# Decode attention with a gated FFN: the last 128 KB of the output weights loaded in rows of 124 and 4

## Chip, cores, metric

One core of a Trainium2 chip. The metric is the device time of one execution in microseconds. Times inside an execution are microseconds from the start of the profile's span.

## The reference, cut

```python
q = (x @ wq)                                   # x: 4 x 512, one decode step, 32 heads of 128
k, v = k_cache[:, :, -4096:, :], v_cache[:, :, -4096:, :]     # 8 KV heads
o = softmax(q k^T / sqrt(128)) v               # cut
a = o.reshape(4, 1, 4096) @ wo                 # wo: 4096 x 512, bf16, 4 MB
b = (relu(x W_gate) * (x W_up)) @ W_down
out = g * a + (1 - g) * b                      # g = sigmoid(x . gate_w)
```

81 MB are read from HBM for four rows of output.

## The kernel before

All loads are issued by SyncE, in one order: `wq`, small inputs, the K and V windows in pieces of 4 MB, the FFN's weights, and at the end `wo` in six pieces, each with a semaphore of its own. A row of `Wo` on a partition is 32 blocks (`i`) of 512 elements (1 KB); a piece `(lo, hi)` is that range of blocks on all 128 partitions.

```python
WO_PIECES = ((0, 8), (8, 16), (16, 24), (24, 28), (28, 30), (30, 32))
# ... in the sync program
elif k == "wo":
    lo, hi = WO_PIECES[it[1]]
    load(("WO", it[1]), f"d_wo{it[1]}", Wo[:, lo:hi, :], A_wo.rearrange("(p i) c -> p i c", i=32)[:, lo:hi, :], waits=w)
# ... in the tensor program: two matmuls per block, accumulated in one bank
def WO(p):
    lo, hi = WO_PIECES[p]
    w = [("WO", p)] + [("E", "OQ", g) for g in range(2)]
    for i in range(lo, hi):
        for j in range(OUTT):
            mm(...)            # cut: oq[:, i, :] against Wo[:, i, 256 j : 256 j + 256]
# ... after the last of them VectorE evicts the bank and SyncE and ScalarE store it
```

## Time and profile before

| | before |
|---|---|
| time, median of 3 runs | 197.48 us |
| span of the profiled run | 195.6 us |
| PE, DVE busy | 62%, 63% |
| DMA | 415 GB/s on average |

Two lines of the page, the span in 40 equal slices of 4.9 us: the busy share of the 16 DMA engines in tenths, and what they moved.

```profile
DMA  6999999999999999999999999999999999999991
GB/s 221 442 423 436 429 442 436 419 436 429 436 456 429 437 426 436 429 429 429 436 429 436 426 429 429 429 429 429 429 426 429 429 405 434 448 429 403 417 402 53
```

From the second slice to the last but one the engines are 90% or more busy. No compute engine comes near that over the span.

The end of the chain of waits (start, length, what):

```profile
173.35 19.49 DMA slots<-in_A_wo_dram
192.84 0.04 issue
192.89 0.40 PE bank L320 x4
193.29 0.02 issue
193.31 0.42 DVE osum L576
```

The last load was issued at 173.35 us and landed at 192.84; everything after it is four short matmuls (0.40 us), one eviction and the store. So what this tail costs is decided by when the **last engine** has delivered.

The DMA view, queues (packets, MB, share of the 16 engines' time) and the loads of `wo` (KB each, us to landing):

```profile
q1 hardware_dynamic: 3904, 81.01, 97.1%
q8 instruction: 6, 0.10, 0.2%
q14 instruction: 1, 0.01, 0.0%
...
slots<-in_A_wo_dram SPq DMA_DIRECT2D x3, 1024.0 KB, 16.4
...
slots<-in_A_wo_dram SPq DMA_DIRECT2D x1, 512.0 KB, 19.2
slots<-in_A_wo_dram SPq DMA_DIRECT2D x2, 256.0 KB, 19.4
```

Besides the loads (q1) there are seven packets that fetch instructions. They look negligible, 0.2%. They are not, for a reason that no average shows.

**From packets to engines.** The packet records have start, duration and size, but no engine. A packet nearly always starts 3 or 4 ns before its predecessor on the same engine ends, so packets can be chained into 16 engines, by a search for the cheapest consistent assignment. Chains are not equally certain: where two run within a few ns of each other they can be swapped. What follows uses only what all best assignments share. Of the kernel before, the start of each engine's last semaphore write (us), with the instruction fetches that its chain holds:

```
ten engines without a fetch         190.46 to 191.11
fetch of  8 KB (q14) at  63.7       191.96
fetches of 16 KB (q8) at 39.1, 72.0, 110.9, 146.0, 182.6     192.11 192.36 192.29 192.24 192.28
```

A chain that took a fetch falls 1.0 to 1.6 us further back, against the middle one, and stays there to the end, within 0.3 us: no engine idles, so none catches up. Only part of that is the fetch's own packet (0.31 us for 8 KB, 0.92 to 1.06 for 16 KB). The 32 KB packet behind it took 1.71 to 1.87 us, where 1.21 is usual (behind the fetch at 182.6 an 8 KB packet, 0.81 instead of 0.31). The landing of 192.84 us belongs to one of those six. (A seventh fetch, at 191.5 us, left no delay in any chain: its engine was through or nearly so.)

### The profile page before, as it was taken

What the parts mean: (1) busy time and instruction counts of PE and PEld (TensorE: products, weight loads), DVE (VectorE), ACT (ScalarE), POOL (GpSimd) and SP (SyncE); (2) the same over time, 40 slices, a digit from 0 to 9 for tenths busy, and PEclk for the clock granted to TensorE, in tenths of its full rate; (3) what the DMA queues carried; (4) which work ended last, traced back from release to release, by engine and by line L of the source; (5) the groups of instructions that cost most, each with busy time, mean ns of one, the idle gap of its engine ahead of it and who ended that gap; (6) DMA issues with size and microseconds to landing.
All of it is one profiled execution on the core that took longest, in us unless ns stands there. A gap on an engine that the chain in (4) does not pass through costs nothing.

```text
span 195.6 us, 1780 instructions
## 1 busy us (share of the span) xinstructions
PE 121.2 (62%) x741; PEld 50.9 (26%) x741; DVE 124.0 (63%) x153; ACT 27.3 (14%) x33; POOL 9.5 (5%) x25
## 2 busy tenths in 40 slices
PE   0418279465933894595468953893395557734954
PEld 0213123122411331142113521241141112412631
DVE  6104769999299819971998199819972997460000
ACT  2213000040130013001300131014001400420100
POOL 7830000000000000000000000000000000000000
PEclk9999957999999697999886999699999789997999
DMA  6999999999999999999999999999999999999991
GB/s 221 442 423 436 429 442 436 419 436 429 436 456 429 437 426 436 429 429 429 436 429 436 426 429 429 429 429 429 429 426 429 429 405 434 448 429 403 417 402 53
DMA packets 3919, 81.12 MB, mean 415 GB/s; under 512 B 572, under 2 KB 584, under 8 KB 968
## 3 DMA queue, kind: packets, MB, share of 16 engines
q1 hardware_dynamic: 3904, 81.01, 97.1%
q8 instruction: 6, 0.10, 0.2%
q14 instruction: 1, 0.01, 0.0%
q10 hardware_dynamic: 8, 0.00, 0.0%
HBM read 81.01 MB, written 0.00 MB: 414 GB/s over the span
## 4 chain that ended last, share of the span: by engine, by line
DMA 54%; DVE 30%; PE 9%; issue 5%; SPq 1%; ACT 0%
DMA slots<-in_A_k_cache_dram 38%; DVE kt L492 21%; DMA slots<-in_A_wo_dram 10%; PE bank L320 7%; DMA gwT<-in_gate_w_dram 6%; DVE sc L528 5%; DVE qblk L518 1%; SPq L256 1%; DVE pT L543 1%; PE bank L324 1%; DVE rd L532 1%; ACT gwB L598 0%; DVE negmax L538 0%; DVE oq L555 0%; DVE osum L576 0%
## 5 line engine op out<-in xcount | busy, mean ns | idle before, releaser
L492 DVE STREAM_TRANSPOSE kt<-slots 128x2048 f32<-128x2048 f32 x32 | 73.7, 2304 | 27.5 <-DMA slots<-in_A_k_cache_dram 27.5
L320 PE MATMUL bank<-kt,qblk 128*128 128x512 bf16 x256 | 71.4, 430 | 29.2 <-DVE kt L492 29.1
L320 PEld LDWEIGHTS bank<-kt,qblk 128*128 128x128 bf16 x256 | 24.9, 106 | 70.7 <-DVE kt L492 37.6
L320 PE MATMUL bank<-slots,pT 128*64 128x512 bf16 x256 | 32.0, 407 | 5.7 <-DMA slots<-in_A_v_cache_dram 5.7
L617 ACT ACTIVATE pe<-sc,negmax 128x2048 bf16<-128x2048 bf16 x8 | 16.0, 2002 | 60.3 <-DVE negmax L538 60.3
L528 DVE CUSTOM_DVE_ANT_0 sc<-bank,maskf 128x512 bf16<-128x512 f32 x32 | 21.1, 658 | 4.1 <-PE bank L320 4.1
L320 PEld LDWEIGHTS bank<-slots,pT 128*64 128x64 bf16 x256 | 15.0, 117 | 23.1 <-issue 13.1
L543 DVE STREAM_TRANSPOSE pT<-pe 128x2048 bf16<-128x2048 bf16 x8 | 18.5, 2312 | 2.2 <-ACT pe L617 2.2
L602 ACT ACTIVATE osb<-bank 128x512 bf16<-128x512 f32 x8 | 4.8, 597 | 81.5 <-PE bank L320 81.5
L320 PE MATMUL bank<-rd,grpb 128*128 128x32 bf16 x8 | 1.5, 192 | 21.0 <-DVE rd L532 19.3
L555 DVE TENSOR_TENSOR oq<-bank,recip 64x128 bf16<-64x128 f32 x2 | 0.9, 442 | 11.5 <-PE bank L320 11.4
L320 PEld LDWEIGHTS bank<-rd,grpb 128*128 128x128 bf16 x8 | 0.8, 97 | 24.7 <-DVE rd L532 22.7
L320 PE MATMUL bank<-slots,oq 128*4 128x256 bf16 x64 | 4.3, 272 | 2.6 <-DMA slots<-in_A_wo_dram 1.9
L496 DVE COPY xT<-bank 128x16 bf16<-128x16 bf16 x1 | 0.2, 167 | 8.2 <-PE bank L324 8.2
L320 PE MATMUL bank<-slots,xT 128*4 128x512 bf16 (+1 forms) x64 | 5.2, 483 | 0.0
L576 DVE CAST osum<-bank 128x256 bf16<-128x256 f32 x1 | 0.4, 425 | 6.5 <-PE bank L320 6.5
L518 DVE TENSOR_SCALAR qblk<-bank 32x64 uint32<-32x64 uint32 x16 | 2.9, 215 | 2.3 <-PE bank L324 2.2
L320 PE MATMUL bank<-maskr,maskl 128*128 128x512 bf16 x1 | 0.6, 609 | 5.9 <-POOL maskr L296 5.9
L324 PE MATMUL bank<-identb,xsb 4*128 4x4 bf16 x4 | 0.3, 166 | 5.4 <-DMA xsb<-in_A_x_dram 5.4
L320 PEld LDWEIGHTS bank<-slots,oq 128*4 128x4 bf16 x64 | 2.3, 83 | 4.4 <-DMA slots<-in_A_wo_dram 3.1
L296 POOL TENSOR_SCALAR_AFFINE_SELECT fold<-fold 128x256 bf16<-128x256 bf16 x8 | 3.3, 417 | 1.1
L487 DVE MEMSET qblk<- 128x2304 uint32 x1 | 2.0, 1978 | 1.4 <-PEq L640 1.4
(58 smaller groups left out, 42.2 us busy)
## 6 DMA issues: line engine op xcount, KB each, us to landing
slots<-in_A_k_cache_dram SPq DMA_DIRECT2D x8, 4096.0 KB, 25.2
slots<-in_A_v_cache_dram SPq DMA_DIRECT2D x8, 4096.0 KB, 30.6
slots<-in_A_wq_dram SPq DMA_DIRECT2D x1, 4096.0 KB, 12.4
slots<-in_A_wo_dram SPq DMA_DIRECT2D x3, 1024.0 KB, 16.4
slots<-in_B_W_gate_dram SPq DMA_DIRECT2D x1, 1792.0 KB, 19.7
slots<-in_B_W_up_dram SPq DMA_DIRECT2D x1, 1792.0 KB, 23.6
slots<-in_B_W_down_dram SPq DMA_DIRECT2D x1, 1792.0 KB, 18.6
slots<-in_A_wo_dram SPq DMA_DIRECT2D x1, 512.0 KB, 19.2
```

The costliest lines, as they stand in the source:

```text
L256: E.op(lambda: e.dma_start(dst, src), ev=ev, waits=waits, ctr=ctr)
L296: op(lambda: e.affine_select(dst, src, pattern, cmp, fill, base=base, channel_multiplier=mult), ev)
L320: E.op(lambda: t.matmul(out_, lhsT, rhs, start=start, stop=stop, tile_position=pos, skip_group_check=True), ev=ev, waits=waits)
L324: E.op(lambda: t.transpose(out_, in_, idn), ev=ev, waits=waits)
L487: E.op(lambda: v.memset(qblk[:, :, :, :, :].rearrange("p s h c e -> p (s h c e)"), 0.0), ev=("QZ",))
L492: E.op(lambda: v.transpose(kt[:, f, :].bitcast(FP32), slot("k", s)[:, 4096 * f:4096 * f + 4096].bitcast(FP32)), ev=("E", "KT", s, f), waits=w)
L518: E.op(lambda dst=dst, r=r, g=g: v.tensor_scalar(dst, src[r, g, 0:B, :, :], 0, None, op0=ALU.bitwise_or), ev=("E",) + keys[1] if (q, g) == ...
L528: E.op(lambda: v.tensor_tensor_reduce(sc[:, 512 * f:512 * f + 512], banks[scb(key)], R["maskf"][:, :], 1.0, -3.0e38, ALU.add, ALU.max, mx4 ...
L532: E.op(lambda: v.tensor_tensor(rd32[:, :, :], bc(R["own8"][:, :].unsqueeze(2), 2, 4), bc(mx4[:, :].unsqueeze(1), 1, 8), ALU.mult), ev=("MA ...
L543: E.op(lambda: v.transpose(pT[:, s % 2, :], pe[:, :]), ev=("E", "PT", s), waits=[("EXP", s)] + ([("PV", s - 2)] if s >= 2 else []))
L602: E.op(lambda: a.activation(osb[:, s % 4, :], ob(s), ACTF.Copy), ev=("NORM", s), waits=[("PV", s)] + ([("OQ", 0)] if s >= 4 else []))
L617: E.op(lambda: a.activation(pe[:, :], sc[:, :], ACTF.Exp, bias=negmax[:, s % 2:s % 2 + 1], scale=SCALE, accum_out=rowsum[:, s:s + 1]), ev= ...
```

## The change

Its intent, as far as the diff tells it: let the last 128 KB be carried by four engines, so that the other twelve, the late ones among them, finish earlier.

```diff
-WO_PIECES = ((0, 8), (8, 16), (16, 24), (24, 28), (28, 30), (30, 32))
+WO_PIECES = ((0, 8), (8, 16), (16, 24), (24, 28), (28, 30), (30, 31), (31, 32))
+LOW4 = (0, 124, 128)
...
+    def wo_rows(p):
+        return [slice(a, b) for a, b in zip(LOW4, LOW4[1:])] if p == len(WO_PIECES) - 1 else [slice(0, 128)]
...
-                load(("WO", it[1]), f"d_wo{it[1]}", Wo[:, lo:hi, :], A_wo.rearrange("(p i) c -> p i c", i=32)[:, lo:hi, :],
-                     waits=w)
+                wo = A_wo.rearrange("(p i) c -> p i c", i=32)
+                for n, r in enumerate(wo_rows(it[1])):
+                    load(("WO", it[1], n), f"d_wo{it[1]}_{n}", Wo[r, lo:hi, :], wo[r, lo:hi, :], waits=w)
...
-            w = [("WO", p)] + [("E", "OQ", g) for g in range(2)]
+            w = [("WO", p, n) for n in range(len(wo_rows(p)))] + [("E", "OQ", g) for g in range(2)]
```

## The prediction

> **What bounds it now.** The page's slices show the DMA engines 90% or more busy from slice 2 to 39 at about 429 GB/s, and the chain of waits ends in the loads of the output weights: 19.5 us from the issue at 173.35 us, then the last four matmuls (0.40 us), the eviction (0.42 us) and the store. So only the moment when the last output weights land counts. DVE and PE (63%, 62% busy) are not the limit there.
>
> **The tail, engine by engine.** The trace records each DMA packet with start, duration and size. A packet starts 3 to 4 ns before its predecessor on the same engine ends, so I chained them into 16 engines. Just before the last 256 KB piece (8 rows of 2 KB each per engine) ten engines are early and six late by about 1 to 1.3 us; they write their last semaphore from 190.46 to 191.11 us (ten) and from 191.96 to 192.36 us (six). The six are those that each served one instruction fetch (16 KB packets near 39, 72, 111, 146 and 183 us, one of 8 KB near 64 us); one fetch puts an engine back by 1.0 to 1.45 us for good. The landing that PE waits for, 192.84 us, is a late engine's.
>
> **What the change does.** The last piece becomes two: 128 KB as before on 16 engines, 128 KB in rows of 124 and 4. The Trainium skill ("DMA: Bandwidth & Descriptors", on why a DMA increments its semaphore by 16) says that a DMA uses the largest number of engines up to 16 that divides its rows, the lowest-numbered ones: 4 for both. The trace agrees for a 4-row load: x has one semaphore update at issue and four at landing.
>
> Costs, from packets: a 2 KB row occupies an engine for 80 ns, a 1 KB row 42 ns (46 less the overlap).
> - Twelve engines: 8 x 80 becomes 8 x 42 ns: 0.30 us earlier.
> - Four lowest: 8 + 31 + 1 rows of 42 ns instead of 8 of 80: 1.68 against 0.64 us, 1.05 us later.
> - Two further issues of 0.43 us end near 174.3 us, 16 us before their data: free. One more wait on PE: free. Last matmuls: two instead of four, some 0.07 us less.
>
> **Critical path.** If all four lowest engines were early ones they would end near 191.8 us, still before the other late ones (192.07), and the kernel would gain 0.3 us. But the chains in which the four 1 KB packets of x lie (the four lowest) include, in every reconstruction that fits, the one of the 8 KB fetch at 64 us, which is late: its second last piece ends at 191.32 us. From there 40 rows take 1.70 us: 193.02 us instead of 192.37 us. So +0.65 us, less 0.07: about +0.6 us on 197.48, **198.1 us**. Range 197.3 to 198.9: lower if no late engine is among the four, higher if a 16 KB fetch has hit one of them too (two of the four are ambiguous), or the fetch at 191.5 us does.
> Chances: faster by over 2% 0.005, within 2% 0.98, slower by over 2% 0.015.
>
> **What will show it.** Landings of the 124-row and the 4-row load: one update group at issue, four at landing, the last near 193.4 to 193.5 us; packets of 1 KB on only four chains after about 192.1 us; all before 189 us unchanged; the last matmul group starts near 193.5 us and has two matmuls.
>
> **What would make it wrong.** Fetches that fall on other engines from run to run; four engines that slow each other (packets well over 46 ns), which would cost up to another microsecond; or 1 KB rows that cost more than x's did.

## The result

| | before | changed |
|---|---|---|
| median (6 runs each) | 197.36 us | 197.89 us |
| lowest to highest | 197.31 to 197.48 | 197.81 to 198.23 |
| span of the profiled run | 195.6 us | 196.2 us |

The ratio is 1.0028, 95% interval 1.0016 to 1.0041. (A ratio is the mean time of one kernel's fast runs over that of the other's fast runs of the same rounds, so not quite the ratio of the medians.) The changed kernel is slower by 0.5 us, and the interval leaves out 1.

The same views of the changed kernel. The slices:

```profile
DMA  6999999999999999999999999999999999999990
GB/s 220 434 429 434 441 434 454 441 431 428 434 428 434 429 428 424 428 428 428 428 428 428 424 434 428 441 428 428 428 444 428 441 400 456 434 404 413 423 370 28
```

Only the end differs, and little can be read from it: a slice is a fortieth of the span, so the last ones begin some 0.6 us later in the changed kernel. Over equal stretches the two move nearly the same: 392 and 387 GB/s from 188 to 190 us, 247 and 243 from 190 to 192, 14 and 11 from 192 to 194. The engines have to be looked at one by one.

The end of the chain of waits:

```profile
174.07 19.42 DMA slots<-in_A_wo_dram
193.49 0.14 issue
193.62 0.29 PE bank L326 x2
193.91 0.02 issue
193.94 0.42 DVE osum L582
```

The last landing is 0.65 us later (193.49 against 192.84), the matmuls behind it are 0.11 us shorter because two are left instead of four, and PE idles 0.14 us after the landing before it starts them, instead of 0.04. The eviction is as long as before.

The DMA view:

```profile
q1 hardware_dynamic: 4040, 81.01, 96.8%
q8 instruction: 6, 0.10, 0.2%
q14 instruction: 1, 0.01, 0.0%
...
slots<-in_A_wo_dram SPq DMA_DIRECT2D x1, 128.0 KB, 19.4
slots<-in_A_wo_dram SPq DMA_DIRECT2D x1, 124.0 KB
...
slots<-in_A_wo_dram SPq DMA_DIRECT2D x1, 4.0 KB
```

The two new loads have no time to landing: the view gives one only for a load with 16 semaphore updates from the engines. These two have one update at issue and four at landing. The landings of the last loads (us), and the last semaphore write of the chains:

```
16-engine load, 128 KB   190.65 ... 192.64   (16 updates)
124 rows                 174.19, then 192.11 192.51 192.59 193.30
4 rows                   183.88, then 192.29 192.68 192.78 193.49

chains with 40 rows of 1 KB at the end, fetch of 8 KB at 64.6   192.87
chains with 40 rows of 1 KB at the end, no fetch                191.57 192.04 192.08
chains with a fetch of 16 KB                                    191.79 to 192.04
other chains                                                    190.09 to 190.83
```

Here the four are certain, since only they carry 1 KB rows to the end. One of them is the late one, and it lands 0.7 us after the other three.

### The profile page after: what moved, and what is told of

Same layout as the page of the kernel before. It is cut to its first block, busy times and chain, and to the rows that moved or that the text cites. A ratio compares the mean times of both kernels' runs of the same rounds, so it can differ in the third digit from the quotient of the medians.

```text
span 196.2 us, 1783 instructions
## 1 busy us (share of the span) xinstructions
PE 124.0 (63%) x741; PEld 52.5 (27%) x741; DVE 124.3 (63%) x153; ACT 27.3 (14%) x33; POOL 9.6 (5%) x25
## 4 chain that ended last, share of the span: by engine, by line
DMA 41%; DVE 31%; PE 19%; issue 6%; SPq 2%; ACT 0%
DMA slots<-in_A_k_cache_dram 25%; DVE kt L498 21%; PE bank L326 17%; DMA slots<-in_A_wo_dram 10%; DMA gwT<-in_gate_w_dram 6%; DVE sc L534 5%; SPq L261 2%; PE bank L330 2%; DVE qblk L524 1%; DVE pT L549 1%; DVE rd L538 1%; DVE negmax L544 0%; ACT gwB L604 0%; DVE oq L561 0%; DVE osum L582 0%
## 5 line engine op out<-in xcount | busy, mean ns | idle before, releaser
L326 PE MATMUL bank<-slots,pT 128*64 128x512 bf16 x256 | 33.4, 420 | 5.7 <-DMA slots<-in_A_v_cache_dram 5.7
L326 PEld LDWEIGHTS bank<-slots,pT 128*64 128x64 bf16 x256 | 15.5, 121 | 23.9 <-issue 14.5
```

Source lines behind the costliest of these rows:

```text
L326: E.op(lambda: t.matmul(out_, lhsT, rhs, start=start, stop=stop, tile_position=pos, skip_group_check=True), ev=ev, waits=waits)
```

## The experiments

E1 to E4 ran on one chip, E5 to E8 on another and E9 on a third, each batch beside runs of the kernel before, whose medians were 197.33, 197.37 and 197.49 us.

### E1: two loads, all 16 engines

```diff
-WO_PIECES = (..., (28, 30), (30, 32))
+WO_PIECES = (..., (28, 30), (30, 31), (31, 32))
```

> The last 256 KB in two loads of 128 KB, both over all 16 engines; nothing goes to four engines alone. My theory (what costs is the 24 KB more that a late one of the four lowest engines has to carry): no loss, 197.2 to 197.45 us against 197.36 before (each engine carries the same bytes; 8 rows of 2 KB become 16 of 1 KB, 16 x 42 against 8 x 80 ns, +0.03 us; two matmuls fewer after the last landing, -0.07 us). Rival 'the extra loads, issues and waits cost': the loss of the change, near 197.9 us, stays.

Measured: 197.24 us (197.16 to 197.36), ratio 0.9996 (0.9983 to 1.0008). Splitting the piece costs nothing. The rival that blames the number of loads and waits falls as the main cause. (E1 tests one further load with its wait; the change has two, and two waits before its last matmuls. Its last issues are far ahead of their data in any case. What the trace shows of the second wait is said below, with the prediction.)

### E2: the four-engine loads earlier

```diff
-WO_PIECES = (..., (24, 28), (28, 30), (30, 31), (31, 32))
+WO_PIECES = (..., (24, 25), (25, 28), (28, 30), (30, 32))
-    ... if p == len(WO_PIECES) - 1 else ...
+    ... if p == 3 else ...
```

> The 124-row and 4-row loads are there, but for row block 24, ahead of 3 KB, 2 KB and 2 KB rows that go over all 16 engines: the same bytes per engine as in the change, but no load of four engines at the end. My theory (an engine's total decides, since it is never idle): as slow as the change, 197.8 to 198.1 us. Rival 'four engines at the end are slow because they are only four, or because a load of four engines lands late': back to 197.3 to 197.5 us.

Measured: 198.55 us (198.4 to 198.8), ratio 1.006 (1.0046 to 1.0073). **Neither theory expected this.** It is not back near 197.4, so the rival falls as stated, but the loss is 1.2 us where equal bytes should give 0.5. "The engine's total decides" cannot be all. The windows of the trace (stretch, its length, busy time of PE, PEld, DVE, ACT, POOL, granted clock, DMA share, GB/s) show what else happened. First the kernel before:

```profile
188.00:190.00 2.00, 0.91 (x18) 0.51 (x12) 0.00 (x0) 0.00 (x0) 0.00 (x0) 1.00 0.98 392
190.00:192.00 2.00, 1.41 (x24) 0.88 (x24) 0.00 (x0) 0.00 (x0) 0.00 (x0) 1.00 0.65 247
```

and E2:

```profile
188.00:190.00 2.00, 1.38 (x26) 0.89 (x20) 0.00 (x0) 0.00 (x0) 0.00 (x0) 1.00 1.01 327
190.00:192.00 2.00, 0.56 (x12) 0.47 (x14) 0.00 (x0) 0.00 (x0) 0.00 (x0) 1.00 0.84 258
192.00:194.00 2.00, 1.79 (x22) 0.58 (x16) 0.00 (x0) 0.00 (x0) 0.00 (x0) 0.67 0.27 99
```

The engines are as busy as ever but deliver 327 instead of 392 GB/s. While the four-engine load ran beside the others, packets grew on all sides: 8 KB from 309 to as much as 476 ns, 3 KB from 121 to 215, 1 KB from 46 to 89. The chain with the 8 KB fetch ended at 193.58 us, 1.2 us after the latest of the kernel before. Some 0.2 us more of this profile's loss is PE's: its last four matmuls took 0.61 us instead of 0.40, at a granted clock of 0.67 from 192 to 194 us. So a load of four engines slowed the 16-engine loads that ran beside it. E6 and E7 ask why.

### E3: twice the amount

```diff
-WO_PIECES = (..., (28, 30), (30, 31), (31, 32))
+WO_PIECES = (..., (28, 30), (30, 32))        # the last piece, 256 KB, still in rows of 124 and 4
```

> The last 256 KB (2 KB rows) on the four lowest engines: each of them 32 rows of 80 ns instead of 8. My theory: the late one of the four ends 1.92 us later than in the kernel before, and is 0.40 us earlier than the latest there: +1.5 us, 198.7 to 199.1 us, and all four end last (the three early ones near 192.6 us on the trace's scale, the late one near 193.9). Rival 'a fixed cost of a four-engine load': as the change, 197.9 us.

Measured: 199.1 us (198.69 to 199.31), ratio 1.0086 (1.0073 to 1.01), at the upper edge of what was expected; the rival that the loss is a fixed cost falls. PE's last groups of matmuls:

```profile
191.85 1.13 PE L326 MATMUL bank<-slots,oq 128*4 128x256 bf16 x12 [0.47 <-DMA slots<-in_A_wo_dram]
194.55 0.49 PE L326 MATMUL bank<-slots,oq 128*4 128x256 bf16 x4 [1.57 <-DMA slots<-in_A_wo_dram]
```

PE idles 1.57 us for the four. Their chains end at 192.54, 192.71, 193.25 and, the one with the 8 KB fetch, 193.85 us. (The three early ones were expected near 192.6; the one at 193.25 missed that by 0.65 us, with packets of 2 KB up to 166 ns. It didn't end last.) The twelve others are through by 191.9.

### E4: marks that number the engines

```diff
+                for n in range(15, 0, -1):       # behind gate_w, rows of 256 B into a scratch tile
+                    load(("MARK", n), f"d_mark{n}", R["mark"][0:n, n - 1, 0:128], A_wo[0:n, 0:128])
```

> The kernel before with 15 small loads of n rows of 256 B (n = 15 down to 1) behind x and gate_w: if a load of n rows uses the n lowest engines, engine e carries 15-e of them, so every chain of packets gets its number. Time as before within 0.3 us. My theory: the chain of the 8 KB fetch near 64 us is one of engines 0 to 3, and the 16 KB fetches fall on engines above 3. It falls if the 8 KB chain carries 11 marks or fewer.

Measured: 198.7 us, one run of unknown state. The time was a miss: the marks of one engine landed about 0.2 us after each other, where I had counted them as nearly free, so the run says nothing about time. For the numbering it serves: a load of n rows shows one semaphore update at issue and n at landing, for every n. The best assignment puts the 8 KB fetch on engine 3 and the 16 KB ones before the last on engines 5, 6, 9, 10, 11. Of those the 8 KB fetch could be forced onto engine 0 at a clearly worse fit, the fetch at 112.6 us onto 8 likewise, and the one at 183.8 us onto 12 at a somewhat worse one. A second search found one more that fits nearly as well as the best: the 16 KB fetch at 147.4 us on engine 1. So by the marks the 8 KB fetch is among the four lowest; that the 16 KB ones are above them rests on the change and on E3 as well, where the four carriers are certain and only one of them has a fetch.

### E5: rows of 123 and 5, so that the late one is spared

```diff
-LOW4 = (0, 124, 128)
+LOW4 = (0, 123, 128)
```

The Trainium skill ("DMA: Bandwidth & Descriptors", section "Why a DMA increments its semaphore by 16 and not by 1") says that the engines used are the largest number up to 16 that divides the rows, and the lowest ones: three for 123 rows, five for 5.

> The change with rows of 123 and 5 in place of 124 and 4: 41 rows of 1 KB go to each of engines 0, 1, 2, then one row to each of engines 0 to 4, so that engine 3, which by the marks has the 8 KB fetch, carries one row of the last 128 KB. My theory (the loss is the late engine among the four): 41 x 42 ns from 190.4 to 190.65 us on the trace's scale, ends 192.1 to 192.5 us beside 192.04 of the late high engines: 197.1 to 197.5 us, the loss of 0.5 us gone although each carrier carries more than in the change. Rival 'a load of few engines at the end costs by itself': 197.9 us or more.

Measured: 197.49 us (197.46 to 197.61), ratio 1.0003 (0.9991 to 1.0016). No loss is left that could be told from zero, although each of the carriers has 41 rows instead of 31. (The change's interval begins where this one ends, at 1.0016; the two were not run side by side, but each beside the kernel before, so the trace has to bear this out.) The trace agrees with the rule: the 123-row load has three engine landings (192.67, 192.76, 192.83), the 5-row load five. The chain with the 8 KB fetch carries exactly one 1 KB row of the last load in every best assignment, so it is engine 3 or 4, and with the four of x it is engine 3. It ends at 191.20, the three carriers at 192.25 to 192.40, the 16 KB late ones at 191.78 to 192.12. The end of the chain of waits:

```profile
174.84 18.17 DMA slots<-in_A_wo_dram
193.01 0.14 issue
193.14 0.29 PE bank L326 x2
193.44 0.02 issue
193.46 0.42 DVE osum L582
```

193.01 instead of the change's 193.49, and 192.84 before. This is the experiment that decides: same bytes, same place in the queue, fewer carriers, and the late engine spared all but one row. No run gave the rows to another late engine on purpose.

### E6: E2, written to partitions of the carriers' own ports (a wrong result)

```diff
+                    if (it[1], n) == (3, 0):
+                        dst = kt[0:13:4, :, :].rearrange("p f x -> p (f x)")[:, 0:31 * 512].rearrange("p (r c) -> p r c", r=31)
+                        src = wo[r, lo, :].rearrange("(e r) c -> e r c", e=4)
```

The Trainium skill ("SBUF — State Buffer", section "Door 1: The DMA port swizzle") gives the write port of every partition and says which engine serves which port in a 128-row load. By it, partitions 0, 4, 8, 12 lie on the ports that engines 0, 1, 2, 3 write anyway, whereas 124 rows run over the ports of all.

> As e2_early4, but the 124 rows go to partitions 0, 4, 8 and 12 of a tile that is free (a wrong result on purpose), 31 rows of 1 KB to one partition per engine, from the same addresses of the same tensor. In e2 every engine's packets grew, 8 KB from 309 to 470 ns, while the four-engine load ran beside the others. If the cause is that the four write into partitions that other engines write at that time, packets stay near 309 ns and the time falls to 197.8 to 198.1 us (the 0.6 us of the engine's extra bytes). If the cause is the reading side, it stays near 198.5 us.

Measured: 197.8 us (197.72 to 197.92), ratio 1.0018 (1.0004 to 1.0032). 8 KB packets in the tail took 309 to 321 ns, 1 KB packets 46 to 60. The windows of E6:

```profile
188.00:190.00 2.00, 1.64 (x30) 1.11 (x26) 0.00 (x0) 0.00 (x0) 0.00 (x0) 1.00 1.00 383
190.00:192.00 2.00, 1.15 (x18) 0.71 (x18) 0.00 (x0) 0.00 (x0) 0.00 (x0) 1.00 0.62 237
```

383 GB/s instead of E2's 327, and the time of the change is back (PE's last four matmuls are at 0.40 us too, at a granted clock of 1.00): the chain with the 8 KB fetch ends last again, at 192.90 us (192.87 in the change).

### E7: E2, read from one contiguous block (a wrong result)

```diff
+                    if (it[1], n) == (3, 0):
+                        src = A_wo[0:124, :].unsqueeze(1)
```

> As e2_early4, but the 124 rows of 1 KB come from one contiguous block of the same tensor instead of rows 32 KB apart (a wrong result on purpose); the partitions written are those of e2. If the slow packets come from the writing side: unchanged, 198.4 to 198.7 us, 8 KB packets up to 470 ns. If they come from the reads: 197.8 to 198.1 us and packets near 309 ns.

Measured: 198.65 us (198.6 to 198.89), ratio 1.0063 (1.0049 to 1.0077), 8 KB packets up to 486 ns. The window of E7:

```profile
188.00:190.00 2.00, 1.35 (x26) 0.89 (x20) 0.00 (x0) 0.00 (x0) 0.00 (x0) 1.00 1.02 320
```

The spacing of the source rows is not the cause. With E6: where the four engines **write** makes the slow packets. That it is the port fits both runs but was not measured by itself; E6 also changed how many partitions are written.

### E8: only the last 64 KB on three engines

```diff
 # on top of E5: block 31's first 256 columns over 16 engines, its last 256 columns in rows of 123 and 5
+[(slice(0, 128), slice(0, OW))] + [(slice(a, b), slice(OW, 512)) for a, b in zip(LOW4, LOW4[1:])]
```

> A try at a kernel better than both: only the last 64 KB (512 B rows) in rows of 123 and 5. By the theory the three early engines end near 191.6 us and the late high ones 0.1 us earlier than before: 197.1 to 197.3 us, hardly to be told from before. If it is above 197.5 us, few-engine loads cost something that the theory lacks.

Measured: 197.27 us (197.22 to 197.42), ratio 0.9992 (0.9979 to 1.0006). It isn't told apart from the kernel before. It is faster than the change, whose interval begins at 1.0016, though the two were not run side by side.

### E9: whose fetch is it

```diff
+            for n in range(20):                  # VectorE, right at its start
+                E.op(lambda n=n: v.memset(R["idle"][0:1, n:n + 1], 0.0))
```

> The changed kernel with 20 tiny writes of VectorE at its start, while the first 12 us of loads run. In both profiles the 8 KB fetch came just when VectorE had 63 of its records behind it. If it is VectorE's instruction stream that is fetched, the fetch moves to VectorE's record 63 here, about 20 records earlier, near 38 to 50 us; it still falls on one of the four lowest engines, that engine still lands last, and the time stays 197.7 to 198.2 us. If the fetch stays near 64 us, it is not VectorE's.

Measured: 198.06 us (197.82 to 198.4), ratio 1.0033 (1.0016 to 1.005). The 8 KB fetch moved from 64.6 to 41.4 us, when VectorE had 64 records behind it (63 before). So it fetches VectorE's instructions. It still falls on one of the four, and that chain ends last, at 192.80 us. In the best assignments of all profiles that can tell (the change, E2, E3, E5 to E9) this fetch is on one of the four lowest engines.

## Why the prediction was right, point by point

- **The bound.** Right. The last landing moved by 0.65 us, PE's last group shortened by 0.11, the median moved by 0.53 (the prediction said 0.6 and 198.1 us).
- **"One more wait on PE: free."** Off by some 0.1 us, which undid what the shorter group gained: PE idled 0.14 us after the landing instead of 0.04. E3 and E5, which also end in two waits, show 0.14, E1 with one wait shows 0.04. Nothing was run to part the waits from the rest.
- **Four engines, the lowest.** Right: one update at issue and four at landing on both loads, and E5 shows that 123 and 5 rows use three and five.
- **A late engine among the four.** Right, and the point that decides: with all four early, the prediction had said a gain of 0.3 us. E5 took the late one out and the loss vanished, but no gain showed: its carriers, with 42 rows each, ended beside the late ones (192.25 to 192.40 us).
- **Its cost.** Near by two errors that partly cancel. Its second last 256 KB ended at 191.01 us and not 191.32, and the 40 rows took 1.87 us instead of 1.70 (to the end of its last semaphore write). The sum, 192.88, was forecast as 193.02: the latest chain ended 0.51 us later, not 0.65. That the landing moved by 0.65 all the same is luck, from a term that the forecast lacked. The last semaphore write landed 0.62 us after it began, against 0.48 before. It is that of the 4-row load, 48 ns behind the one of the 124-row load on the same engine, and the two landed 0.19 us apart (0.17 to 0.19 on all four engines, as the list of landings shows; E4's marks had been 0.2 apart). So the separate 4-row load seems to cost some 0.14 us that its bytes don't show; no run took it away. Thirty-one rows took 1.46 us where 31 x 42 ns is 1.30, as its packets grew to 82 ns between 191.36 and 191.84.
- **The three early ones.** Forecast near 191.8 us; they ended at 191.57, 192.04 and 192.08. The same slow packets, up to 92 ns. "Four engines that slow each other" stood among what could make the prediction wrong; it happened in small. E2, E6 and E7 show the thing in large, beside 16-engine loads, and tie it to where the four write. That the slow packets of the change have this cause is likely, not shown.
- **The twelve others.** Forecast to end at 192.07, measured 192.04.
- **Issues free.** Right in effect, wrong in detail: the issue of the 4-row load took 9.60 us, not 0.43, and ended at 183.67. It cost nothing only because its data came 9 us later. Why it waits was not looked into.
- **Unchanged before 189 us.** On the DMA side, yes: the third 1 MB piece landed at 190.17 against 190.34. PE ran the FFN's last group 0.95 us later in the changed kernel's profile, at 184.61 instead of 183.66, off the chain that ended last.

What stays open: whether the write port as such makes the slow packets (E6 and E7 show only that it is where the four write), what holds up the long issue, and what one load and one wait less at the end would save.

## What to carry to other kernels

When DMA is saturated to the end, the kernel ends with its latest engine, so a share of work moved between engines must be judged by each engine's own lateness, not by the mean: chain the packets and look who is late before choosing who carries the rest. A row count decides how many of the lowest engines take part, and one row more or less (124 or 123) can put the late one in or out. A load over few engines is best not laid beside loads over all of them: put ahead of 896 KB of such loads (E2), it cost 1.2 us instead of 0.5.

## What the Trainium skill lacked or had wrong

- "Runtime: NRT & Kernel Launch", section "Instruction fetch mechanics", calls the cost of crossing a block of instructions mostly hidden. Whether it was for the engine that executes them was not looked at; but the fetch is a packet on one of the 16 DMA engines that carry the loads, and it put that engine back by 1.0 to 1.6 us until the end.
- The same section has refills of 16 KB. VectorE's was one packet of 8 KB (on q14), when VectorE had 63 records behind it. Those on q8 were 16 KB (six of them); they came every 190 to 290 records of PE, so they are probably PE's, which no run tested.
- "DMA: Bandwidth & Descriptors" says how many engines a load uses, and not that a load over few engines can slow loads from HBM over 16 that run beside it (what it has on back-pressure is of transfers between cores): 392 GB/s fell to 327, 8 KB packets went from 309 to 476 ns (E2), and stayed at 309 to 321 with other destination partitions (E6).
- No page that I read tells that an issue can hold up the issuing queue for long when few-engine loads are queued: 9.60 us for the 4-row load of the change, 7.95 in E3, 10.06 for the 5-row load of E5, against 0.33 to 0.43 for each load of `wo` in the kernel before.
